# Attention and token MLP on one core: when GpSimd gets its turn on the port that it shares with VectorE

## Chip, cores and metric

The kernel runs on one core of one Trainium2 chip. The metric is the device time in microseconds of one execution; the time of a kernel is the median of several runs. Five engines work beside each other: TensorE (PE in the profile, its weight loads PEld), VectorE (DVE), ScalarE (ACT), GpSimd (POOL) and SyncE (SP), which issues the DMAs.

## What is computed

The input x is 2048 x 512 in bf16. It is normalized by rows once (`xn`). The output is x plus two terms of it:

```python
xn  = layernorm(x)
# A: full attention, 32 heads of 16 elements, 2048 queries and keys
p   = softmax(q @ k.T * 16 ** -0.5);  A = concat(p @ v) @ wo
# B: a token MLP (2048 -> 1376 -> 2048) over the transposed, once more normalized xn
u   = gelu(einsum("bsd,sf->bdf", layernorm(xn), w1) + b1)
B   = (einsum("bdf,fs->bds", u, w2) + b2).T
out = x + A + B
```

The bulk of the work is the exponential of 32 x 2048 x 2048 scores, 134 million of them.

## The kernel before

**Tiles.** The scores are cut into 1024 tiles of 128 keys x 1024 columns (two heads times 512 queries). For each tile TensorE makes the scores (line 798) into two PSUM banks, one engine takes the exponential into a buffer (`pT`, or a part of `x_sb` that has come free), and TensorE multiplies the buffer by the values (line 880). Sums and products are gathered in one PSUM bank for 32 tiles (a block), then copied out (line 1102), divided and projected.

**Two ways to the exponential.** Most tiles go to ScalarE, which has an exponential (line 824). The others go to VectorE: one pass adds a constant to the scaled score and writes it as an int16 that is read as bf16 (`dexp`, line 833, PSUM to SBUF). Its error is taken down by three more copies of the buffer, each shifted by another constant (`SHIFTS`, line 839, int16, SBUF to SBUF); all four are multiplied by the values and summed in PSUM. So a tile on VectorE costs one `dexp`, three shifts and four products where a tile on ScalarE costs one exponential and one product. Each of the three shifts can run on VectorE (`shd`) or on GpSimd (`shp`). A `dexp` or an exponential is written as one record of 1024 columns where the two banks are neighbours, else as two of 512.

**The order.** Nothing of the order is written out by hand. When the program is built, a planner (`Sched` and the loop that ends the kernel function) keeps a modelled clock of each engine, lists what could be issued next on every engine with an estimated start (`est`), and adds the earliest. Costs are pairs: the time until the engine takes its next instruction, and the time until the result is there (`SH_I, SH_L = 1.11, 1.05` for a shift on GpSimd, `TS_I, TS_L = 0.335, 0.42` for one on VectorE). A semaphore is taken as `SEM = 0.05`. What the planner added becomes each engine's instruction stream, with the semaphore waits that the dependencies need.

**Choices of the planner.** Eight numbers steer it (`POLICIES`, 36 rows), among them `d_steal`, the lead that lets a tile go to VectorE, and `p_slack`. `PLAN` names one row of them for each 16 tiles, 64 in all. A piece of work is a candidate for GpSimd only if the next moment at which VectorE could want the port lies far enough behind the estimated start on GpSimd:

```python
pl = [z for z in pl if max(dve_port, sc.free["dve"]) - z[0] >= z[4] - p_slack]
```

`z[0]` is the estimated start and `z[4]` the length that is asked for (`SH_I` for a shift, 1.25 for other GpSimd work).

**The port.** Shifts on VectorE, one late multiply on VectorE and all computing instructions on GpSimd are marked as users of one port. In the model VectorE's marked instruction starts no earlier than the start of GpSimd's last one plus its issue time, and GpSimd's no earlier than the end of the issue time of VectorE's last one plus `POOL_AFTER = 0.03` (`port_time`). In the program GpSimd's instruction also gets a dependency on VectorE's last marked instruction (`port_op`): it waits on a semaphore until that one has finished. VectorE has no wait in the other direction.

Of the kernel before, what the change touches and what calls it, by code (L numbers as in the profile page):

```python
# [58 lines left out]
SEM = 0.05  # L59
PE_SWITCH = 0.10  # L60
PE_LAT = 0.38
PV_T = 0.1095
POOL_AFTER = 0.03
AS_I, AS_L = 0.8, 0.9
EXP_I, EXP_L = 0.904, 1.03
EXPH_I, EXPH_L = 0.477, 0.60
# [16 lines left out]
SH_I, SH_L = 1.11, 1.05  # L83
# [12 lines left out]
PLAN_STEP = 16  # L96
PLAN = tuple(int(c, 36) for c in "00f41j96ioe4283j88076r8jjti283fos8rs08tig23g0ih10n7tg0i05608f5v6")
URGENT = ("kv0", "qt", "kt", "vt")
URG_DUE = 24
UT0, UT_STEP = 196, 31  # L100
# [8 lines left out]
class Op:  # L109
# [3 lines left out]
    def __init__(self, eng, fn, name=""):  # L113
        self.eng = eng
        self.fn = fn
        self.pos = -1
        self.deps = []
        self.signals = False
        self.waits = []
        self.is_dma = False  # L120
        self.dma_sem = None
        self.dma_val = 0
        self.q = None
        self.after = None
        self.name = name
        self.t0 = 0.0
        self.t1 = 0.0


class Sched:  # L130
    ENGS = ("pe", "act", "dve", "pool", "sp")

    def __init__(self, nc, es):
        self.nc = nc
        self.es = es
        self.streams = {e: [] for e in self.ENGS}
        self.order = []
        self.last_writer = {}
        self.readers = {}
        self.dma_ops = []  # L140
        self.free = {e: 0.0 if e in ("sp", "act") else 0.7 for e in self.ENGS}
        self.busy = {e: 0.0 for e in self.ENGS}
        self.pe_mode = None
        self.pe_end = 0.0
        self.pe_tiles = {}
        self.port_free = {"dve": 0.0, "pool": 0.0}
        self.port_op = None
        self.act_end = 0.0
        self.pe_work = []
        self.filler = None  # L150
        self.pend = []
# [85 lines left out]

    def port_time(self, eng, t):

        return max(t, self.port_free["pool"] if eng == "dve" else self.port_free["dve"] + POOL_AFTER)  # L240

    def _time(self, op, cost, ready, port):
        eng = op.eng
        if port:
            ready = self.port_time(eng, max(self.free[eng], ready))
        if op.is_dma:
            op.t0 = max(self.free[eng], ready)
            self.free[eng] = op.t0 + cost[0]
            op.t1 = op.t0 + cost[1]
        elif eng == "pe":  # L250
            mode, tiles, dur = cost
            t = max(self.free["pe"], ready)
            if mode != self.pe_mode:
                t = max(t, self.pe_end + PE_SWITCH)
                self.pe_mode = mode
                self.pe_tiles = {}
            for x in tiles:
                t = max(t, self.pe_tiles.get(x, 0.0))
            for x in tiles:
                self.pe_tiles[x] = t + dur  # L260
            self.pe_end = max(self.pe_end, t + dur)
            self.free["pe"] = t + 0.004
            self.busy["pe"] += dur * len(tiles) / 4.0
            op.t0, op.t1 = t, t + dur + PE_LAT - 0.214
            self.pe_work.append((t, dur, len(tiles) / 4.0))
        else:
            op.t0 = max(self.free[eng], ready)
            self.free[eng] = op.t0 + cost[0]
            self.busy[eng] += cost[0]
            op.t1 = op.t0 + cost[1]  # L270
            if eng == "act":
                op.t1 = max(op.t1, self.act_end + cost[0] + (EXP_GAP if op.name == "exp" else 0.0))
                self.act_end = op.t1
                self.free[eng] = max(self.free[eng], op.t1 - ACT_QUEUE)
        if port:
            self.port_free[eng] = op.t0 + cost[0]

    def add(self, eng, fn, reads=(), writes=(), name="", dma=False, out_dma=False, cost=None, port=None):
        op = Op(eng, fn, name)
        op.is_dma = dma  # L280
        op.q = "o" if out_dma else "i"
        if cost is None:
            cost = (DMA_I, DMA_L) if dma else (("F", (0, 1, 2, 3), 0.22) if eng == "pe" else (EV_I, EV_L))
        deps = self._deps(eng, reads, writes, dma)
        deps.discard(op)
        if port is None:
            port = eng == "pool" and not dma
        ready = self.ready(eng, reads, writes, dma)
        if eng == "pe" and self.filler is not None:
            self.pend = [k[1] for k in writes if k[0] == "bank"] if name == "sc" and cost[2] > 0.2 else []  # L290
            self.keep_clock(ready, cost)
        self._time(op, cost, ready, port)
        if port and eng == "pool" and self.port_op is not None:
            deps.add(self.port_op)
        if port and eng == "dve":
            self.port_op = op
        op.deps = list(deps)
        for k in reads:
            self.readers.setdefault(k, []).append(op)
        for k in writes:  # L300
            self.last_writer[k] = op
            self.readers[k] = []
        op.pos = len(self.streams[eng])
        self.streams[eng].append(op)
        self.order.append(op)
        if dma:
            self.dma_ops.append(op)
        return op
# [79 lines left out]
def bass_parallel_sum__softmax_full_mha__mixer_token_mlp__prompt_kernel(  # L388
# [18 lines left out]
    with ExitStack() as es:  # L407
# [415 lines left out]
        def exp_specs(n):  # L823
            return [dict(eng="act", fn=lambda e, cs=cs, src=src: e.activation(buf(pbuf[n])[:, cs], src, ACTF.Exp, scale=LN2_128),  # L824
                         reads=[("bank", k) for k in ks], writes=half_keys(free_p[0], cs), name="exp",
                         cost=(EXP_I, EXP_L) if side(n) else (EXPH_I, EXPH_L)) for cs, src, ks in parts(n)]
# [5 lines left out]
        def dexp_spec(n, w):  # L832
            return [dict(eng="dve", fn=lambda e, cs=cs, src=src: e.tensor_scalar(  # L833
                buf_i(w)[:, cs], src, IBIAS, 0.0, ALU.add, ALU.max),
                reads=[("bank", k) for k in ks], writes=half_keys(w, cs), name="dexp",
                cost=(P1_I, P1_L) if side(n) else (P1H_I, P1H_L)) for cs, src, ks in parts(n)]
# [491 lines left out]
        def h_ok():  # L1328
            return next_n >= H_AT + H_STEP * h_n[0] and all(("xT", t) in have for t in range(NT))
# [45 lines left out]
        def est(specs):  # L1375
            s0 = specs[0]
            r = 0.0
            for s_ in specs:
                r = max(r, sc.ready(s_["eng"], s_["reads"], s_["writes"]))
            t = max(sc.free[s0["eng"]], r)  # L1380
            if s0.get("port"):
                t = sc.port_time(s0["eng"], t)
            return t
# [102 lines left out]
        while True:  # L1486
            if next_n >= plan_at and plan_at < NN:
                d_steal, p_keep, dead_slack, pe_fit, ext_rank, d_back, d_fly, p_slack = POLICIES[PLAN[plan_at // PLAN_STEP]]
                plan_at += PLAN_STEP
# [11 lines left out]
            if ready_q and free_p:  # L1501
                el = []
                for n in ready_q:
                    sp_ = exp_specs(n)
# [6 lines left out]
            if ready_q and fly < d_fly and len(free_p) >= 4 + p_keep:  # L1511
                act_free = sc.free["act"]
                for qi, n in enumerate(ready_q):
                    if NN - n <= D_END:
                        continue
                    sp_ = dexp_spec(n, free_p[0])
                    t = est(sp_)
# [6 lines left out]
            for j in sh_jobs:  # L1524
                if j["ok"]():
                    sp_ = shift_spec("dve", j["w"], j["o"], j["k"])
# [11 lines left out]
            pl = []  # L1538
            dve_port = min([z[0] for z in dl if z[2] == "shd" or (z[2] == "gen" and z[3]["cur"][1][0].get("port"))] + [1e9])
            for j in sh_jobs:  # L1540
                if NN - j["n"] <= POOL_END:
                    continue
                sp_ = shift_spec("pool", j["w"], j["o"], j["k"])
                pl.append((est([sp_]), 1, "shp", (j, sp_), SH_I))
            for g in frees + exts:
                if g["cur"] and g["cur"][0] == "pool":
                    pl.append((est(g["cur"][1]), 0, "gen", g, 1.25))
            if hgen is not None and h_ok():
                pl.append((max(sc.free["pool"], next_h), 2, "h", None, 0.67))
            pl = [z for z in pl if max(dve_port, sc.free["dve"]) - z[0] >= z[4] - p_slack]  # L1550
# [6 lines left out]
            sp_, e_s = None, 1e9  # L1557
# [3 lines left out]
            if next_n < NN and pv_grp >= grp(vblk(next_n)) - 1 and len(free_banks) >= 2 + spare and score_has(next_n):  # L1561
                s_ = best_pair()
                banks_of[next_n] = s_
                sp_ = score_specs(next_n)
# [44 lines left out]
            if not cands:  # L1609
                pl = [z for z in ([] if not sh_jobs else [(0, 0, "shd", (sh_jobs[0], shift_spec("dve", sh_jobs[0]["w"], sh_jobs[0]["o"], sh_jobs[0]["k"])))])]  # L1610
# [12 lines left out]
            elif kind == "exp":  # L1623
                n, sp_ = what
                ready_q.remove(n)
                exp_commit(n)
                for z in sp_:
                    add(z)
                free_banks.extend(banks_of[n])
            elif kind == "dexp":  # L1630
                n, sp_ = what
# [3 lines left out]
                for z in sp_:  # L1635
                    add(z)
# [8 lines left out]
            elif kind in ("shd", "shp"):  # L1645
                j, sp_ = what
# [15 lines left out]
            elif kind == "gen":  # L1662
                g = what
# [9 lines left out]
            elif kind == "score":  # L1673
                n, sp_, s_ = what
# [6 lines left out]
            elif kind == "pv":  # L1681
# [4 lines left out]
                if pv_left[b] == 0:  # L1686
                    g = dict(gen=task_spill() if b < 0 else task_epilogue(b) if b < NBLK - 1 else task_tail(b - NBLK + 1), cur=None)
# [4 lines left out]
            elif kind == "ext":  # L1692
                g = what
# [21 lines left out]
            for i, (rel, due, nm, gen, need) in enumerate(ext_tasks):  # L1715
# [19 lines left out]
                g = dict(gen=gen, cur=None, due=due, name=nm)  # L1735
# [63 lines left out]
```

## Time and profile before

| what | value |
|---|---|
| median of 3 runs | 699.4 us (699.33 to 699.7) |
| profiled execution, whole time | 698.69 us |
| its span, first to last instruction | 696.9 us |
| granted TensorE clock | 1.000 |
| busy: PE, DVE, ACT, POOL | 686.0, 664.7, 678.5, 388.0 us |
| shifts on POOL (line 839) | 303 records, 1043 ns each |
| shifts on DVE (line 839) | 609 records |
| `dexp` on DVE (line 833) | 233 of 1024 columns, 142 of 512 |

The whole time of the profiled execution is 1.8 us over its span and 0.7 us under the median of the runs. A group of the profile names line, engine, operation, what is written and read, the number of records, busy time and mean duration, then the idle time of the engine just before these records and what ended most of it. Records of one engine overlap by some 85 ns, since an instruction starts before the one ahead has written its last results: a shift on VectorE has a record of 420 ns and the next instruction starts 334 ns after it.

### The profile page before, as it was taken

How to read it: one execution, taken by the hardware profiler on the slowest of the kernel's cores; microseconds unless marked ns; L12 is line 12 of the kernel's file. 1: busy time of each engine (PE TensorE's matmuls, PEld its weight loads, DVE VectorE, ACT ScalarE, POOL GpSimd, SP SyncE). 2: the span in 40 equal slices, each digit the busy share in tenths (PEclk: the TensorE clock that was granted, in tenths of full speed). 3: DMA queues.
4: the chain of work that ended last, by engine and by line, in shares of the span. 5: the costliest groups of instructions: out<-in, count | busy, mean ns of one | idle time of the engine just before them, and what ended most of it. 6: DMA issues, size and time to landing. Idle time of an engine off the chain costs nothing.

```text
span 696.9 us, 30015 instructions
## 1 busy us (share of the span) xinstructions
PE 686.0 (98%) x13235; PEld 317.9 (46%) x13235; DVE 664.7 (95%) x1198; ACT 678.5 (97%) x789; POOL 388.0 (56%) x436
## 2 busy tenths in 40 slices
PE   8999999999999999999999999999999999999998
PEld 6544444444444444444444444444444444444444
DVE  7888979989999999998999999999999999989997
ACT  7999999999999999999999999999999999999996
POOL 6856744355565556555555565555555545545644
PEclk9999999999999999999999999999999999999999
DMA  7410140101222121221122213120220202112101
GB/s 227 68 24 12 50 83 20 30 3 32 43 47 57 40 59 41 49 56 35 28 49 63 59 30 81 45 50 27 48 61 24 49 23 64 46 46 62 41 26 46
DMA packets 88756, 33.86 MB, mean 49 GB/s; under 512 B 70514, under 2 KB 88626, under 8 KB 88626
## 3 DMA queue, kind: packets, MB, share of 16 engines
q1 hardware_dynamic: 87810, 31.56, 19.6%
q8 instruction: 103, 1.69, 1.0%
q10 hardware_dynamic: 816, 0.39, 0.2%
q14 instruction: 27, 0.22, 0.1%
HBM read 21.70 MB, written 2.35 MB: 35 GB/s over the span
## 4 chain that ended last, share of the span: by engine, by line
PE 66%; DVE 23%; ACT 9%; issue 2%; POOL 0%; DVEq 0%; POOLq 0%
PE ps L880 23%; PE ps L798 23%; PE ps L928 16%; DVE pT L833 9%; ACT pT L824 7%; DVE pT L839 6%; DVE x_sb L833 3%; DVE x_sb L839 2%; ACT x_sb L824 2%; PE ps L984 1%; DVE OT L1102 1%; PE ps L869 0%; DVE Qall L954 0%; DVE osb L1076 0%; PE ps L721 0%
## 5 line engine op out<-in xcount | busy, mean ns | idle before, releaser
L824 ACT ACTIVATE pT<-ps 128x1024 bf16<-128x1024 f32 (+1 forms) x570 | 528.5, 1106 | 5.4 <-PE ps L798 4.6
L798 PE MATMUL ps<-QT,KT 32*128 32x512 bf16 x1976 | 276.0, 385 | 1.9 <-DVE pT L833 0.4
L833 DVE TENSOR_SCALAR pT<-ps 128x1024 int16<-128x1024 f32 (+1 forms) x265 | 264.1, 1013 | 9.9 <-PE ps L798 9.6
L880 PE MATMUL ps<-pT,V 128*32 128x256 bf16 x4624 | 245.1, 275 | 1.4 <-DVE OT L1102 0.3
L839 POOL TENSOR_SCALAR pT<-pT 128x1024 int16<-128x1024 int16 x158 | 164.8, 1043 | 124.2 <-DVE pT L839 86.6
L824 ACT ACTIVATE x_sb<-ps 128x1024 bf16<-128x1024 f32 (+1 forms) x197 | 201.3, 1089 | 1.2 <-PE ps L798 1.2
L798 PEld LDWEIGHTS ps<-QT,KT 32*128 32x128 bf16 x1976 | 76.9, 91 | 169.8 <-ACT pT L824 72.8
L880 PEld LDWEIGHTS ps<-pT,V 128*32 128x32 bf16 x4624 | 111.5, 96 | 73.7 <-issue 52.7
L839 DVE TENSOR_SCALAR pT<-pT 128x1024 int16<-128x1024 int16 x317 | 129.4, 434 | 0.4
L833 DVE TENSOR_SCALAR x_sb<-ps 128x1024 int16<-128x1024 f32 (+1 forms) x110 | 110.9, 1024 | 2.7 <-PE ps L798 1.8
L880 PE MATMUL ps<-x_sb,V 128*32 128x256 bf16 x1712 | 109.2, 275 | 0.4 <-DVE x_sb L839 0.3
L839 POOL TENSOR_SCALAR pT<-x_sb 128x1024 int16<-128x1024 int16 x64 | 66.8, 1043 | 50.0 <-DVE pT L839 39.0
L839 POOL TENSOR_SCALAR x_sb<-pT 128x1024 int16<-128x1024 int16 x57 | 59.5, 1043 | 37.7 <-DVE pT L839 26.8
L880 PE MATMUL ps<-pT,VM 128*32 128x256 bf16 x912 | 64.8, 275 | 0.9 <-POOL VM L687 0.5
L928 PE MATMUL ps<-hx,wblk 128*32 128x512 bf16 x688 | 59.9, 384 | 0.0
L880 PEld LDWEIGHTS ps<-x_sb,V 128*32 128x32 bf16 x1712 | 43.8, 96 | 25.4 <-issue 19.5
L839 DVE TENSOR_SCALAR pT<-x_sb 128x1024 int16<-128x1024 int16 x133 | 54.5, 432 | 0.2
L839 DVE TENSOR_SCALAR x_sb<-pT 128x1024 int16<-128x1024 int16 x110 | 46.1, 426 | 0.1
L928 PE MATMUL ps<-wkv_raw,wblk 128*32 128x512 bf16 x512 | 44.7, 385 | 0.0
L1141 POOL TENSOR_TENSOR oT<-oC,denb 128x256 bf16<-128x256 f32 (+1 forms) x32 | 23.3, 729 | 31.0 <-DVE pT L839 16.2
L839 POOL TENSOR_SCALAR x_sb<-x_sb 128x1024 int16<-128x1024 int16 x24 | 25.0, 1043 | 18.5 <-DVE pT L839 15.6
L880 PEld LDWEIGHTS ps<-pT,VM 128*32 128x32 bf16 x912 | 24.2, 96 | 15.6 <-issue 9.7
(124 smaller groups left out, 462.3 us busy)
## 6 DMA issues: line engine op xcount, KB each, us to landing
wblk<-in_B_w_dram SPq DMA_DIRECT2D x10, 512.0 KB, 4.6
wblk<-in_B_w_dram SPq DMA_DIRECT2D x16, 320.0 KB, 3.6
oC<-OT SPq DMA_DIRECT2D x248, 16.0 KB, 2.2
denb<-rden_scratch SPq DMA_DIRECT2D x124, 32.0 KB, 1.9
xr<-in_A_x_dram SPq DMA_DIRECT2D x16, 128.0 KB, 2.4
out_dram<-osb SPq DMA_DIRECT2D x16, 128.0 KB, 2.0
QT<-Qall SPq DMA_DIRECT2D x120, 16.0 KB, 1.8
x_sb<-in_A_x_dram SPq DMA_DIRECT2D x2, 512.0 KB
```

The source lines that it names most:

```text
L798: specs.append(dict(eng="pe", fn=lambda e, r=r, bk=bk: e.matmul(bank(bk), lhsT=KT[32 * r:32 * r + 32, T, 128 * kt:128 * (kt + 1)], rhs=QT[ ...
L824: return [dict(eng="act", fn=lambda e, cs=cs, src=src: e.activation(buf(pbuf[n])[:, cs], src, ACTF.Exp, scale=LN2_128), reads=[("bank", k) ...
L833: return [dict(eng="dve", fn=lambda e, cs=cs, src=src: e.tensor_scalar(buf_i(w)[:, cs], src, IBIAS, 0.0, ALU.add, ALU.max), reads=[("bank" ...
L839: return dict(eng=eng, fn=lambda e: e.tensor_scalar(buf_i(o), buf_i(w), float(SHIFTS[k]), 1.0, ALU.add, ALU.mult), reads=[("pT", w), ("pTh ...
L880: specs.append(dict(eng="pe", fn=lambda e, c=c, h=h, i=i, off=off: e.matmul(bank(pv_bank[vb])[32 * c:32 * c + 32, 256 * par:256 * par + 25 ...
L928: specs.append(dict(eng="pe", fn=lambda e, c=c, w=w: e.matmul(bank(ex)[32 * c:32 * c + w, :], lhsT=lhs_of(32 * c, 32 * c + w), rhs=rhs, st ...
L984: specs.append(dict(eng="pe", fn=lambda e, ct=ct, c=c, i=i, t=t: e.matmul(bank(ex)[32 * c:32 * c + 32, 128 * i:128 * (i + 1)], lhsT=xnT[:, ...
L1102: yield "pvev", [dict(eng="dve", name="pvev", fn=lambda e: e.tensor_copy(OT32[:, eb, :], bank(pv_bank[b])), reads=[("bank", pv_bank[b])], ...
L1141: yield "pool", [dict(eng="pool", fn=lambda e, cs=cs: e.tensor_tensor(oT[0:m, qb % NOT, T, cs], oC32[0:m, tb_, cs], denb[0:m, tb_, cs], AL ...
```

## The change

Three things change together.

- GpSimd's dependency moves. When a port user is added on VectorE and the model has it starting right behind the instruction in front of it (less than 0.03 us after VectorE was free), GpSimd's next instruction depends on that instruction in front, and not on the port user itself. Otherwise it depends on the port user as before. VectorE's stream is in order, so the instruction in front ends first.
- The model's times of the port change. GpSimd may start 0.05 + 0.03 us after the end of the instruction that it depends on, and no earlier than 0.165 us (`PORT_EARLY`) before the port user's issue time is over. VectorE may start 0.14 us (`PORT_DVE`) before GpSimd's result is there: 0.91 us after the start of a GpSimd shift, where it was 1.11. The length that a candidate for GpSimd must find free goes from 1.11 to 0.91 for a shift and from 1.25 to 1.05 for other work.
- `PLAN` is another table: 61 of its 64 entries differ.

```diff
-POOL_AFTER = 0.03
+POOL_AFTER, PORT_EARLY, PORT_DVE = 0.03, 0.165, 0.14
...
-PLAN = tuple(int(c, 36) for c in "00f41j96ioe4283j88076r8jjti283fos8rs08tig23g0ih10n7tg0i05608f5v6")
+PLAN = tuple(int(c, 36) for c in "0u389ydi80tnddje715t8t8z40i0d08h0n2h5fuv8188so0yz7xncr0rf83ij8o0")
...
     def port_time(self, eng, t):
-        return max(t, self.port_free["pool"] if eng == "dve" else self.port_free["dve"] + POOL_AFTER)
+        if eng == "dve":
+            return max(t, self.port_free["pool"])
+        if self.port_dep is not None:
+            t = max(t, self.port_dep.t1 + SEM + POOL_AFTER)
+        return max(t, self.port_free["dve"] - PORT_EARLY)
...
         if port:
-            self.port_free[eng] = op.t0 + cost[0]
+            self.port_free[eng] = op.t0 + (cost[0] if eng == "dve" else cost[1] - PORT_DVE)
...
+        was_free = self.free[eng]
         self._time(op, cost, ready, port)
-        if port and eng == "pool" and self.port_op is not None:
-            deps.add(self.port_op)
+        if port and eng == "pool" and self.port_dep is not None:
+            deps.add(self.port_dep)
         if port and eng == "dve":
-            self.port_op = op
+            st = self.streams["dve"]
+            self.port_dep = st[-1] if st and op.t0 - was_free < 0.03 else op
...
-                pl.append((est([sp_]), 1, "shp", (j, sp_), SH_I))
+                pl.append((est([sp_]), 1, "shp", (j, sp_), SH_L - PORT_DVE))
...
-                    pl.append((est(g["cur"][1]), 0, "gen", g, 1.25))
+                    pl.append((est(g["cur"][1]), 0, "gen", g, 1.05))
```

More of the change, by code (lines that the diff above doesn't have):

```diff
@@ L146, in __init__ @@
         self.port_free = {"dve": 0.0, "pool": 0.0}
-        self.port_op = None
+        self.port_dep = None
         self.act_end = 0.0
```

## The prediction

> **What bounds the kernel now.** I began with the busy times by stage (the table of windows: busy time of each engine, PE, PEld, DVE, ACT, POOL in that order, then granted clock, DMA share and GB/s).
>
> ```profile
> 20.00:160.00 140.00, 136.64 (x2964) 66.96 (x2966) 126.88 (x239) 139.18 (x175) 79.98 (x105) 1.00 0.17 36
> 160.00:660.00 500.00, 498.61 (x9316) 221.92 (x9314) 490.67 (x856) 495.32 (x560) 277.63 (x274) 1.00 0.20 47
> 660.00:696.90 36.90, 32.97 (x670) 16.44 (x662) 32.08 (x59) 28.87 (x32) 17.59 (x19) 1.00 0.13 37
> ```
>
> Through 500 of the 697 us ScalarE is busy for 99% and VectorE for 98%; GpSimd has 222 us free. TensorE shows 99.7%, but the ends of its records are modelled and overlap, so I asked the waits who holds it up:
>
> ```profile
> PEld ps L798 <- ACT pT L824: 72.8, 284, 0.5
> PEld ps L798 <- DVE pT L833: 28.3, 104, 0.5
> PEld ps L798 <- ACT x_sb L824: 22.0, 86, 0.4
> PEld ps L798 <- DVE x_sb L833: 12.6, 46, 0.5
> ```
>
> The weight loads of the scores waited 136 us in sum for exponentials to free their banks. So TensorE waits for ScalarE and VectorE together, although the chain that ended last gives it 66%. The time is the exponentials that these two must share: it falls if VectorE can take more tiles, and VectorE can if it loses fewer microseconds elsewhere. The groups show where it spends them:
>
> ```profile
> L833 DVE TENSOR_SCALAR pT<-ps 128x1024 int16<-128x1024 f32 x163 | 198.7, 1219 | 7.2 <-PE ps L798 6.8
> L839 DVE TENSOR_SCALAR pT<-pT 128x1024 int16<-128x1024 int16 x317 | 129.4, 434 | 0.4
> L839 POOL TENSOR_SCALAR pT<-pT 128x1024 int16<-128x1024 int16 x158 | 164.8, 1043 | 124.2 <-DVE pT L839 86.6 <-DVE x_sb L839 30.1 <-DVE pT L833 3.4
> ```
>
> 304 tiles went to VectorE (233 whole, 142 halves); of their 912 shifts 609 ran on VectorE and 303 on GpSimd. GpSimd's idle time ends almost always with a VectorE shift: that is the turn on the port.
>
> **The price of VectorE time.** Start to start, a `dexp` of 1024 columns takes VectorE 1.133 us, a shift 0.334, an exponential ScalarE 0.903 (medians of the records). A tile moved from ScalarE to VectorE, with two of its shifts there, costs VectorE 1.133 + 2 x 0.334 = 1.80 and frees 0.903 on ScalarE. Both are full, so f us freed on VectorE let f / (1.80 + 0.903) more tiles move, and the time falls by 0.903 of that: f / 3.0. Within 0.2% (1.4 us) of the time before is what a measurement of this kernel can't tell from no change.
>
> **The handoff as traced.** The usual cycle (timeline of GpSimd, then of VectorE; start, duration):
>
> ```profile
> 399.71 1.04 POOL L839 TENSOR_SCALAR x_sb<-pT 128x1024 int16<-128x1024 int16 x1 [0.76 <-DVE pT L839]
> 401.51 1.04 POOL L839 TENSOR_SCALAR x_sb<-x_sb 128x1024 int16<-128x1024 int16 x1 [0.76 <-DVE pT L839]
> ...
> 400.68 0.75 DVE L839 TENSOR_SCALAR pT<-x_sb 128x1024 int16<-128x1024 int16 x2
> 401.35 1.22 DVE L833 TENSOR_SCALAR pT<-ps 128x1024 int16<-128x1024 f32 x1
> ```
>
> The two shifts end at 401.43, GpSimd begins at 401.51: 82 ns, as for 254 of its instructions after 20 us. In 248 of these the shift had followed its predecessor without a pause (starts overlap ends by 85 ns), and the predecessor's end lay 333 to 338 ns earlier (10th to 90th percentile) than the semaphore used now. So **the wait moves by 0.334 us**, and GpSimd arrives 0.168 us after VectorE's shift has begun, while it runs.
>
> What happens to one that arrives so is in the trace, where other GpSimd work came in during a shift (GpSimd's row, then VectorE's):
>
> ```profile
> 47.40 0.75 POOL L687 TENSOR_SCALAR VM<-V 128x544 bf16<-128x544 bf16 x1 [0.78 <-DVE V L994]
> ...
> 47.23 0.42 DVE L839 TENSOR_SCALAR pT<-pT 128x1024 int16<-128x1024 int16 x1
> ```
>
> It arrived 168 ns into the shift and took 748 ns; the median of that line is 644. Another (line 634, at 85.19) took 792 against 692. VectorE's shifts kept 0.42 us. So arriving early stretches GpSimd's record by 0.10 us and costs VectorE nothing. A GpSimd shift, counted from the start of VectorE's shift, now ends at 0.42 + 0.082 + 1.043 = 1.545 us and would end at 0.168 + 1.043 + 0.10 = 1.311: 0.234 earlier.
>
> In the other direction, the 28 VectorE shifts with records over 440 ns all started under a running GpSimd instruction and ended 278 to 284 ns after it: as if they began 0.14 before its end. That is the new `PORT_DVE`; the old model had VectorE wait 0.2 us too long. These 28 lost 8.9 us.
>
> **Window sums.** Between two VectorE shifts lies other work, a window. A GpSimd shift fits one without holding VectorE up if the window is 1.545 - 0.14 - 0.334 = 1.07 us long now, and 0.84 after; each further shift needs 1.123 (back to back, median). I cut VectorE's records after 25 us into their 608 windows (375 GpSimd instructions are in them).
>
> - *Blocked shifts.* 14 of the 28 stood behind a GpSimd chain whose first instruction had the 82 ns handoff; ending 0.234 sooner takes off some 0.2 us each: 2.8 us of VectorE. All 28: 6.2. None: 0.
> - *Room without blocking.* The windows hold 346 GpSimd shifts by the old need and 356 by the new: 10 shifts leave VectorE, 10 x 0.334 = 3.3 us. If the planner finds none: 0.
> - *Room with a short block.* If VectorE may be held up by 0.25 us the windows hold 404, that is 48 more, nearly all in windows of one 0.6 us copy. Each blocks 0.84 - 0.60 = 0.24 and saves 0.334, 0.10 net. The new filter lets these in (with slack 0.5 it asks for 0.41 us; the copy gives 0.77), the old one did not (0.61 asked, 0.58 given). Not each will have a shift at hand; I take a third: 1.6 us. Ends 0 and 4.8.
> - *The moved wait itself:* 0.33 us earlier on an engine with 222 us free is worth nothing on the path, and nothing is queued behind it on GpSimd but the next such piece (it issues no DMA). Cover is that idle time; without it each handoff would gain 0.234.
> - *More products:* each tile that moves adds three sets of four products on TensorE, about 0.11 us a set; for 3 tiles 1 us. I cost it at nothing because the score loads wait 136 us for exponentials; if that cover is gone, 1 us is added.
>
> Sum: 2.8 + 3.3 + 1.6 = 7.7 us of VectorE, 2.6 us of time. The profiled execution would go from 698.69 to 696.1; it lay 0.7 under the median, so the median would be 696.8. By the ends: half of the first term alone, 0.5 us (698.9); all at their upper ends 14.3 / 3.0 = 4.8 us (694.6).
>
> **Rivals.**
>
> 1. *GpSimd let in too eagerly* (slower). With slack 0.8 the new filter asks for 0.11 us; one VectorE shift ahead already gives 0.165, so GpSimd may take the port with no other VectorE work as cover. VectorE is then free at 0.334 and the port at 1.311 - 0.14 = 1.17: blocked 0.84, saved 0.334, 0.50 lost. Four of the table's 64 entries have slack 0.8: 64 tiles, some 19 on VectorE, so up to 9.5 us. With slack 0.5 a reciprocal (16 in the kernel, 0.26) suffices: 0.24 lost each, 3.9 us. Together 4.5 us of time, less 2.6 gained: 701.3. It decides from some 15 such turns on (7.7 / 0.50). Against: the planner prices the block and takes a `dexp` instead where scores lie ready. Chance 0.12.
> 2. *The port is held until VectorE's shift has fully ended* (no gain, or slower). GpSimd's work then begins no earlier than now, the window need stays at 1.07, and the planner is 0.23 too hopeful: first term 0; 10 x (0.334 - 0.23) = 1.0; 16 x (0.10 - 0.23) = -2.1, or -6.2 for all 48. Time 699.8 to 701.1. Against: the row at 47.40, whose work ended 500 ns after the shift's end where it needs 644, so it began 144 ns before that end. Chance 0.06. The Trainium skill has this rule (SBUF — State Buffer, section "A bandwidth-pool intuition that's wrong (but worth ruling out)"): GpSimd blocked by VectorE goes on about 115 ns after VectorE's end, measured on descriptor writing. By that figure, an estimate, the new handoff would be 33 ns worse than the 82 of now, and the sum nothing or below; this trace disagrees, by those 144 ns.
> 3. *The reordering opens other waits* (slower). 61 table entries differ, so every later choice differs. After 20 us VectorE has 48 waits over 100 ns, 23.3 us, mostly for scores and projections; half as many again is 11.7 / 3.0 = 3.9 us: 700.7. A third fewer would give 694.2. Chance of the bad side 0.12.
> 4. *No change.* GpSimd starts earlier and idles later, the planner moves no shifts: 699.4. For it: GpSimd already had 222 us free and left them. Chance 0.10.
>
> GpSimd overtaking the shift it should follow would block VectorE for 0.9 us, but needs VectorE's shift to start over 82 ns after its predecessor; none of 609 started more than 36 ns after. No chance of its own.
>
> **Numbers.** The forecast, with its better side, has 0.60: 696.8. Slower is rivals 1, 2 and 3, 0.30; same is rival 4, 0.10. The range goes from 692.5 (all upper ends and most of a third fewer waits: 694.6 - 2.1) to 701.3 (rival 1), with 1 in 10 beyond each.
>
> **What would show it.** Right: GpSimd's shifts begin about 0.17 us after a VectorE shift's start, with records near 1.14 us; over 303 of them; more than 304 tiles on VectorE and fewer ScalarE exponentials; records over 440 ns on VectorE losing less than 8.9 us. Rival 1 shows as many records near 1.2 us on VectorE's shifts; rival 2 as GpSimd records near 1.3; rival 3 as VectorE idle time well over 30 us in sum (30.0 now). I am wrong if shifts move to GpSimd and the tiles on VectorE do not grow, or if ScalarE is no longer 99% busy between 160 and 660 us.

## The result, and the profile after

| | before | changed |
|---|---|---|
| median | 699.37 us | 703.6 us |
| ratio, 95% interval | | 1.006 (1.0048 to 1.0073) |
| span of the profiled execution | 696.9 us | 702.2 us |
| shifts on GpSimd / VectorE | 303 / 609 | 344 / 568 |
| tiles on VectorE | 304 | 304 |
| VectorE shifts with records over 440 ns (blocked), time lost | 28, 8.9 us | 68, 23.0 us |
| VectorE idle, from the span's start to its last instruction | 30.0 us | 34.6 us |
| whole exponentials on ScalarE, mean start to start | 665, 930.3 ns | 679, 936.7 ns |

The kernel became 0.6% slower. (Blocked time is what a record has over 418 ns, summed.) The same table of windows as before, of the changed kernel:

```profile
20.00:160.00 140.00, 136.38 (x2970) 66.55 (x2974) 130.42 (x242) 138.38 (x173) 94.85 (x117) 1.00 0.17 35
160.00:660.00 500.00, 495.18 (x9274) 219.19 (x9266) 482.44 (x777) 494.21 (x542) 325.27 (x301) 1.00 0.20 47
660.00:702.20 42.20, 37.79 (x770) 18.04 (x770) 38.57 (x71) 34.67 (x39) 23.38 (x23) 1.00 0.12 32
```

GpSimd, the fifth engine of each row, works 48 us more between 160 and 660 us; TensorE, VectorE and ScalarE all work less there. What GpSimd took over did not turn into more work of the others. (The busy time of TensorE is modelled; that of the other engines is recorded.) The groups of the changed kernel, as before by line, engine and shape:

```profile
L839 DVE TENSOR_SCALAR pT<-ps 128x1024 int16<-128x1024 f32 x173 | 210.2, 1215 | 4.4 <-PE ps L804 4.2
L845 DVE TENSOR_SCALAR pT<-pT 128x1024 int16<-128x1024 int16 x292 | 127.5, 461 | 0.9
L845 POOL TENSOR_SCALAR pT<-pT 128x1024 int16<-128x1024 int16 x174 | 192.3, 1105 | 92.0 <-DVE pT L845 52.2 <-DVE x_sb L845 18.4 <-PE ps L804 7.7
```

VectorE's shifts went from 317 to 292 in this group, but their mean from 434 to 461 ns, so they cost nearly the same. GpSimd's mean went from 1043 to 1105 ns. The timeline shows both (GpSimd's rows, then VectorE's):

```profile
82.66 1.04 POOL L845 TENSOR_SCALAR pT<-x_sb 128x1024 int16<-128x1024 int16 x1
84.06 1.15 POOL L845 TENSOR_SCALAR pT<-x_sb 128x1024 int16<-128x1024 int16 x1 [0.36 <-DVE pT L845]
...
81.96 1.21 DVE L839 TENSOR_SCALAR pT<-ps 128x1024 int16<-128x1024 f32 x1
83.09 1.22 DVE L845 TENSOR_SCALAR pT<-x_sb 128x1024 int16<-128x1024 int16 x2
84.23 1.21 DVE L839 TENSOR_SCALAR x_sb<-ps 128x1024 int16<-128x1024 f32 x1
```

The two shifts at 83.09 take 1.22 us where two free ones take 0.75: the first stands behind GpSimd's instruction of 82.66 to 83.70. The second then lets GpSimd in at 84.06, and that record is 1.15 us. Of 344 GpSimd shifts 206 arrived 0.14 to 0.26 us into a VectorE shift; their median record is 1.152 us.

Who held up the score loads (waits: total, number, longest):

```profile
PEld ps L804 <- ACT pT L830: 56.7, 212, 0.5
PEld ps L804 <- DVE pT L839: 30.8, 96, 0.8
PEld ps L804 <- ACT x_sb L830: 21.1, 83, 0.4
PEld ps L804 <- DVE x_sb L839: 18.3, 55, 0.6
```

For ScalarE they waited 77.8 us instead of 94.8, for VectorE 49.1 instead of 40.9. And the chain that ended last, by engine, of the kernel before and of the changed one:

```profile
PE 66%; DVE 23%; ACT 9%; issue 2%; POOL 0%; DVEq 0%; POOLq 0%
```

```profile
PE 54%; DVE 33%; ACT 6%; POOL 5%; issue 2%; POOLq 0%; DVEq 0%
```

VectorE's share rose from 23 to 33%, GpSimd's from 0 to 5%. So VectorE now runs late, and ScalarE waits for scores: a whole exponential usually starts 0.904 us after a whole one ahead of it. One that started over 20 ns later than that was released by a score matmul 76 times before (14.1 us of delay) and 118 times now (18.1 us). In the mean whole exponentials start 6.4 ns further apart, 679 x 6.4 = 4.3 us of the 5.3 us of the span. That the scores were late because VectorE freed their banks late is argued from the waits and the chain; it was not followed from score to score.

### The profile page after: what moved, and what is told of

The parts are those of the page before. It is cut to its first block, busy times and chain, and to the rows that moved or that the text cites. A ratio compares the mean times of both kernels' runs of the same rounds, so it can differ in the third digit from the quotient of the medians.

```text
span 702.2 us, 30075 instructions
## 1 busy us (share of the span) xinstructions
PE 687.0 (98%) x13283; PEld 316.8 (45%) x13283; DVE 665.4 (95%) x1132; ACT 681.5 (97%) x775; POOL 455.5 (65%) x477
## 4 chain that ended last, share of the span: by engine, by line
PE 54%; DVE 33%; ACT 6%; POOL 5%; issue 2%; POOLq 0%; DVEq 0%
PE ps L886 19%; PE ps L804 19%; PE ps L934 14%; DVE pT L839 13%; DVE pT L845 8%; DVE x_sb L839 6%; ACT pT L830 4%; DVE x_sb L845 2%; PE ps L990 1%; ACT x_sb L830 1%; POOL pT L845 1%; POOL mv L1246 1%; DVE OT L1108 1%; POOL hx L1251 1%; PE ps L708 0%
## 5 line engine op out<-in xcount | busy, mean ns | idle before, releaser
L830 ACT ACTIVATE pT<-ps 128x1024 bf16<-128x1024 f32 (+1 forms) x549 | 505.2, 1045 | 5.4 <-PE ps L804 4.5
L839 DVE TENSOR_SCALAR pT<-ps 128x1024 int16<-128x1024 f32 (+1 forms) x245 | 256.0, 1058 | 8.9 <-PE ps L804 8.7
L845 POOL TENSOR_SCALAR pT<-pT 128x1024 int16<-128x1024 int16 x174 | 192.3, 1105 | 92.0 <-DVE pT L845 52.2
L830 ACT ACTIVATE x_sb<-ps 128x1024 bf16<-128x1024 f32 (+1 forms) x204 | 208.1, 1068 | 2.2 <-PE ps L804 2.0
L839 DVE TENSOR_SCALAR x_sb<-ps 128x1024 int16<-128x1024 f32 (+1 forms) x105 | 116.2, 1114 | 6.2 <-PE ps L804 5.7
L845 POOL TENSOR_SCALAR pT<-x_sb 128x1024 int16<-128x1024 int16 x83 | 91.3, 1100 | 45.0 <-DVE pT L845 26.8
L845 POOL TENSOR_SCALAR x_sb<-pT 128x1024 int16<-128x1024 int16 x64 | 71.3, 1114 | 35.2 <-DVE pT L845 22.7
L845 DVE TENSOR_SCALAR pT<-x_sb 128x1024 int16<-128x1024 int16 x142 | 60.6, 453 | 0.3
L886 PEld LDWEIGHTS ps<-x_sb,V 128*32 128x32 bf16 x1720 | 43.9, 96 | 27.4 <-issue 20.9
L934 PE MATMUL ps<-hx,wblk 128*32 128x512 bf16 x688 | 56.0, 384 | 0.0
L845 DVE TENSOR_SCALAR x_sb<-pT 128x1024 int16<-128x1024 int16 x97 | 40.8, 432 | 0.2
L886 PEld LDWEIGHTS ps<-pT,VM 128*32 128x32 bf16 x904 | 24.0, 96 | 14.8 <-issue 9.7
```

Source lines behind the costliest of these rows:

```text
L845: return dict(eng=eng, fn=lambda e: e.tensor_scalar(buf_i(o), buf_i(w), float(SHIFTS[k]), 1.0, ALU.add, ALU.mult), reads=[("pT", w), ("pTh ...
L886: specs.append(dict(eng="pe", fn=lambda e, c=c, h=h, i=i, off=off: e.matmul(bank(pv_bank[vb])[32 * c:32 * c + 32, 256 * par:256 * par + 25 ...
L934: specs.append(dict(eng="pe", fn=lambda e, c=c, w=w: e.matmul(bank(ex)[32 * c:32 * c + w, :], lhsT=lhs_of(32 * c, 32 * c + w), rhs=rhs, st ...
```

## Experiments

Three theories. **S**: the planner's new port times are 0.10 us too hopeful. `PORT_EARLY` 0.165 says that GpSimd's work starts when its instruction arrives; on the chip the record is stretched (1.152 against 1.043), so each order planned with it has VectorE late. **T**: the rules are sound and the new table is a bad pick. **W**: the moved wait itself costs time. The runs were taken in several sessions, in which the kernel before had medians of 699.4 to 699.9 us; a difference between sessions is good to about 0.5 us.

### The moved wait alone, in the order of before

```diff
# before.py, planned times untouched, so the order is untouched
-            deps.add(self.port_op)
+            deps.add(self.port_dep)
...
+            self.port_dep = st[-1] if st and op.t0 - was_free < 0.03 else op
```

> The order of before, instruction by instruction, with nothing changed but the semaphore that GpSimd waits for (the VectorE instruction in front of the port's last user). Theory W (the moved wait itself costs): 702 us or more, with VectorE's shift records longer. Theories S and T: 698 to 699.6 us; GpSimd arrives about 0.17 us after a shift's start, its records are near 1.15 us instead of 1.043, their ends come about 0.23 us sooner, and the 8.9 us of blocked VectorE time fall to 5 to 8 us.

Measured: 699.65 us against 699.7, ratio 0.9996 (0.9984 to 1.0008). 221 GpSimd shifts arrived under a VectorE shift (median 0.168 us in, record 1.155, end 1.323 us after that shift's start). Blocked VectorE time fell from 8.9 to 6.1 us. The groups:

```profile
L842 DVE TENSOR_SCALAR pT<-pT 128x1024 int16<-128x1024 int16 x317 | 128.5, 431 | 0.4
L842 POOL TENSOR_SCALAR pT<-pT 128x1024 int16<-128x1024 int16 x158 | 177.9, 1126 | 109.7 <-DVE pT L842 64.9 <-DVE x_sb L842 27.0 <-DVE pT L836 5.4
```

Same counts as before; GpSimd's mean is 83 ns longer, VectorE's 3 ns shorter. W falls: it asked for 702 us or more. By the interval the wait alone is worth between 1.1 us of gain and 0.6 us of loss.

### The old wait, in the order of the changed kernel

```diff
# after.py, order untouched
-            deps.add(self.port_dep)
+            deps.add(self.port_op)      # VectorE's last port user itself
...
+            self.port_op = op
```

> The order of the changed kernel, instruction by instruction, with GpSimd waiting for the port user itself again. GpSimd's records are 1.043 us once more, but start 0.33 us and end 0.23 us later. Theory W: faster than the changed kernel by 2 us or more, under 701.6 us. Theory S (the order has no room for the port's later release): blocked time of VectorE rises over the 23.0 us of the changed kernel to 30 us or more, and the time to 705 to 715 us. Theory T: somewhat over 703.6 us.

Measured: 715.89 us, ratio 1.0226 (1.021 to 1.0241); 69 blocked shifts, 33.7 us.

```profile
L847 DVE TENSOR_SCALAR pT<-pT 128x1024 int16<-128x1024 int16 x292 | 133.0, 479 | 0.9
L847 POOL TENSOR_SCALAR pT<-pT 128x1024 int16<-128x1024 int16 x174 | 182.4, 1048 | 106.4 <-DVE pT L847 72.5 <-DVE x_sb L847 20.8 <-PE ps L806 3.8
```

GpSimd's records are short again (1048 ns), so the stretch belongs to arriving under a shift. But each end comes later, VectorE's mean rises from 461 to 479 ns, and with 10.7 us more blocking the kernel took 12.3 us more. W falls again (it asked for under 701.6 us); S had the blocked time right and the time 0.9 us too low at its upper end. This order has no slack at the port: what the port is late there, the kernel is late.

### Tables and rules exchanged

The changed rules with the old table, and the old rules with the new table (only the `PLAN` line is exchanged).

> The change with the table of before. Theory S (the planner doesn't know that a GpSimd instruction which arrives under a VectorE shift takes 0.10 us longer; it packs VectorE's shifts too tightly behind GpSimd, and they block): the blocked time of VectorE's shifts stays far over the 8.9 us of before, 18 us or more, and the time is over that of the changed kernel, 705 to 712 us, since this table was not chosen for the new rules. Theory T (the new table is a bad pick, the rules are sound): about 697 to 700 us. Theory W (the moved wait itself costs time on the chip, whatever the order): 703 us or more, not told apart here.

> The kernel before with the table of the change, the wait and the port times as they were. Theory T (the table is the cause): 703 to 705 us. Theory S: the blocked time of VectorE's shifts stays near 9 us (under 14), and the time says only that a table fits the rules it was chosen under: 704 to 712 us. Theory W: nothing in particular.

Measured: 711.27 us (1.0162, 1.0145 to 1.0179; 75 blocked shifts, 25.5 us) and 711.34 us (1.0167, 1.0152 to 1.0182; 30 blocked, 9.4 us). T expected 697 to 700 us of the first and 703 to 705 of the second; both miss. S has both inside its ranges, of time and of blocked time. Each table is better under the rules that it came with: by 12 us under the old ones (711.34 to 699.7), by 7.7 under the new (711.27 to 703.6). So a comparison of rules needs a table chosen for neither.

### One row for all 64 places, three sets of rules

```diff
# after.py; in before.py the PLAN line alone
-PLAN = tuple(int(c, 36) for c in "0u389ydi80tn...")
+PLAN = tuple(int(c, 36) for c in "0000000000...")     # then "8888888888..."
# third set only
-POOL_AFTER, PORT_EARLY, PORT_DVE = 0.03, 0.165, 0.14
+POOL_AFTER, PORT_EARLY, PORT_DVE = 0.03, 0.06, 0.14
```

> The rules of before (old wait, old port times) with a flat table: row 0 of the policies in all 64 places, so that no table was picked for any rules. It is the base of the next two: some 707 to 712 us, with VectorE's shifts blocked for 5 to 15 us.

> The changed rules (moved wait, PORT_EARLY 0.165) with the same flat table. Theory S (the turn is planned 0.10 us too early, since GpSimd's record is 1.15 us where it arrives under a shift and the planner has 1.05): 709 to 715 us, not faster than the flat table under the rules of before by more than 1 us, VectorE blocked for 18 us or more. Theory T (the rules are sound and only the table is a bad pick): 2 to 5 us faster than the flat table under the rules of before, 704 to 708 us.

> As the one before with one number changed: PORT_EARLY 0.06 instead of 0.165, so that the planner has GpSimd's instruction begin 0.105 us later behind a VectorE shift, which is what its record is stretched by. Theory S: 2 to 8 us faster than with 0.165, 704 to 709 us, and 1 us or more faster than the flat table under the rules of before. Theory T: within 1.5 us of the run with 0.165.

> A second draw of the flat comparison, since any change of a planned time reorders all that follows: row 8 of the policies in all 64 places, with the rules of before. Base of the next two: 707 to 713 us.

> Row 8 in all places with the changed rules (PORT_EARLY 0.165). Theory S (the turn is planned 0.10 us too early): within 2 us of the same table under the rules of before, or slower. Theory T (the rules are sound, the new table a bad pick): 2 us or more faster than it. VectorE blocked for 18 us or more in both.

> As the one before with PORT_EARLY 0.06. Theory S: faster than with 0.165 by 2 us or more, as it was by 3.0 us with row 0. If that difference was the chance of one reordering: anything from 3 us slower to 3 us faster.

| flat table | rules of before | changed, 0.165 | changed, 0.06 |
|---|---|---|---|
| row 0, us | 710.79 | 711.6 | 708.62 |
| row 0, ratio to the kernel before | 1.0161 (1.0144 to 1.0178) | 1.0171 (1.0156 to 1.0186) | 1.0136 (1.0119 to 1.0153) |
| row 8, us | 713.4 | 715.82 | 710.74 |
| row 8, ratio | 1.0196 (1.0181 to 1.0211) | 1.023 (1.0213 to 1.0247) | 1.0161 (1.0146 to 1.0176) |
| VectorE blocked, row 0 / row 8, us | 11.7 / 10.2 | 20.9 / 18.4 | 18.9 / 16.7 |
| tiles on VectorE, row 0 / row 8 | 298 / 307 | 301 / 317 | 296 / 315 |

With 0.165 the rules bring nothing or a loss (row 8, +2.4 us); 0.105 us later in that one number takes 3.0 and 5.1 us off. T would have had the rules with 0.165 2 us or more ahead of those of before; neither draw shows that. Row 8 under the rules of before came out 0.4 us over the range expected of it. The blocked time fell by only 2 us each: with 0.06 VectorE is still blocked for longer than under the old rules, but when it was meant to be (the planned blocking stands in the table below). The chain that ended last changes in row 8. With 0.165:

```profile
PE 45%; DVE 44%; ACT 3%; POOL 3%; issue 3%; SPq 1%; DMA 1%; DVEq 0%; POOLq 0%
```

and with 0.06:

```profile
PE 46%; DVE 26%; ACT 24%; POOL 2%; issue 2%; DVEq 0%; POOLq 0%
```

VectorE carries 44% and ScalarE 3% in the first; in the second they have 26 and 24%, though 315 tiles run on VectorE against 317. In row 0 it is not so: VectorE's share rises there from 23 to 30% with 0.06. The row 0 gain over the rules of before (2.2 us) has intervals that touch; in row 8 (2.7 us) they do not.

### The number mended, and a table chosen for it

`PORT_EARLY` 0.06 as above and another table, chosen by the planner's own end.

> The changed kernel with PORT_EARLY 0.06 and a table chosen anew for that value, by the planner's own end alone, on no chip. The planner ends it 0.4 us later than it ends the changed kernel with its table. Theory S (a turn planned 0.10 us too early is what the changed kernel loses): faster than the changed kernel's 703.6 us by 2 us or more, 697 to 701.5 us, although it is planned to end later. Theory T (only the choice of table counts): 703.5 to 705 us, as the planner's end says. Whether it beats the 699.4 us of before is open between 697 and 701.

Measured: 699.71 us, ratio to before 0.9998 (0.9989 to 1.0007): 3.9 us under the changed kernel. 333 shifts on GpSimd, 301 tiles on VectorE, 64 blocked shifts with 19.0 us, whole exponentials 926.6 ns apart. Its windows row and chain:

```profile
160.00:660.00 500.00, 498.35 (x9238) 216.84 (x9236) 484.31 (x798) 497.85 (x554) 315.50 (x291) 1.00 0.21 47
```

```profile
PE 63%; DVE 21%; ACT 12%; POOL 1%; issue 1%; POOLq 0%; DVEq 0%
```

ScalarE is busy for 497.9 of 500 us (494.2 in the changed kernel), and VectorE's share of the chain is back from 33 to 21%. T is out: planned to end 0.4 us later, it ends 3.9 us sooner. It is level with the kernel before, not better; no kernel run here is faster than that one by more than can be told.

Laying VectorE's starts in each trace beside the starts that the planner had given the same instructions shows the cause as a lag (median of those planned for 625 to 650 us). The same can be done for the blocked shifts, since the planner's clocks say which shifts it let the port hold up.

| kernel | planned end of VectorE, us | shifts blocked, planned / traced, us | lag, us |
|---|---|---|---|
| before | 693.6 | 11.3 / 8.9 | 0.05 |
| before, with the new table | 706.0 | 12.9 / 9.4 | 0.8 |
| row 0, rules of before | 704.0 | 16.9 / 11.7 | 2.0 |
| row 8, rules of before | 704.4 | 13.5 / 10.2 | 3.8 |
| changed (0.165) | 692.5 | 14.8 / 23.0 | 5.9 |
| changed, with the old table | 699.4 | 18.2 / 25.5 | 6.6 |
| row 0, 0.165 | 703.5 | 18.5 / 20.9 | 2.7 |
| row 8, 0.165 | 702.2 | 13.6 / 18.4 | 8.1 |
| row 0, 0.06 | 702.2 | 19.2 / 18.9 | 2.1 |
| row 8, 0.06 | 702.5 | 19.6 / 16.7 | 2.6 |
| 0.06 and a table of its own | 692.9 | 19.8 / 19.0 | 2.0 |

With 0.165 the chip blocks VectorE longer than planned in all four orders; with 0.06 and under the old rules the sums are below the plan in every order. Row 8 shows it most plainly: 0.165 and 0.06 are planned to end 0.3 us apart, and on the chip they are 5.1 us apart the other way. In row 0 the lags differ by only 0.6 us, so there most of the 3.0 us came with the other order that the planner then chose. The changed kernel was planned to end 1.1 us sooner than the one before and lags 5.9 us: 4.8 us, of which 4.2 were measured.

The lag is 1.7 us with only the wait moved and 15.6 with only the wait moved back. It is that of one execution, and good to about 1 us: the profiled execution with only the wait moved took 0.75 us more than its median, and 0.8 us of its lag was there within the first 45 us.

The old rules were wrong in both directions: GpSimd's start 0.14 us too early, VectorE's release behind GpSimd 0.2 us too late. Together they planned the release 1.475 us behind the start of VectorE's shift where it came at 1.405, 0.07 us too late. The change mended the second error and turned the first into another: 1.08 planned, 1.178 traced, 0.10 us too early.

## Why the prediction was wrong

The kernel was to become 0.4% faster and became 0.6% slower. The first of the two signs of being wrong came: 41 shifts moved to GpSimd and the tiles on VectorE stayed 304. The second did not: ScalarE is still 99% busy between 160 and 660 us.

**The handoff was right.** Arrival 0.168 us into the shift (measured 0.166), record 1.14 us (1.152), end 1.311 us after the shift's start (1.318), VectorE's shift unharmed (417 ns). With the wait alone the blocked time lost 2.8 us, the first term of the sum.

**Rival 2** (the port held to the shift's end) is out: that end at 1.318 leaves 0.142 us of GpSimd's 1.043 before VectorE's record ends at 0.417. The 115 ns behind VectorE's end that the Trainium skill states (SBUF — State Buffer, section "A bandwidth-pool intuition that's wrong (but worth ruling out)"), measured there on descriptor writing, don't hold for this pair of instructions.

**The term that failed is the room with a short block.** I let 26 shifts leave VectorE, 16 of them for 0.24 us of blocking each, and took 2.8 us of blocking off elsewhere: 7.7 us freed. 41 left, 41 x 0.334 = 13.7 us, and blocking rose by 14.1 us (8.9 to 23.0). In the place of +7.7 stands -0.4. Of the 68 blocks 35 cost more than the 0.334 us that a shift saves. Part of it the planner took on knowingly: it planned 14.8 us of blocking, where my terms make 9.9 (8.9 - 2.8 + 16 x 0.24); the other 8.2 us it did not plan. (The sign of less than 8.9 us that I gave for being right did not agree with these terms.)

**A term was missing.** My own sum had GpSimd's end at 1.311 us behind the shift's start; the rules of the diff plan it at 0.17 + 1.05 = 1.22. I priced a planner that is too hopeful in rival 2 (there by 0.23 us) and put this gap of 0.09 at nothing in the forecast, where about 200 instructions meet it. With the reordering that comes with it, mending it is worth 3.0 and 5.1 us under the flat tables, and 3.9 with a table of its own. With the order held, in the planner's own clocks: the changed kernel's order, timed once more with 0.06, ends 3.2 us later (695.78 against 692.54); row 8's ends 4.5 and row 0's 1.6 us later. That is a sum of the model and not a run, and it puts the changed kernel 2.2 us behind the 693.6 of before.

**f / 3.0 was no rule for a fixed order.** VectorE time freed behind the planner's back bought no time that can be told (moved wait alone: 2.8 us freed; the 0.9 us of the rule lie inside that interval, so they are not ruled out), while time lost there is paid in full and not by a third (old wait in the new order: 10.7 us, 12.3 of time). Only the planner turns freed time into tiles, and it had none to turn: 304 tiles before and after. It had itself planned a gain of only 1.1 us.

**Rival 1** (GpSimd let in too eagerly) named the right sign and the right victim, at 701.3 us, but not the place: its blocks of 0.84 us in four stretches of the table do not exist. The longest is 0.74, the mean 0.34, and the changed table has as many entries with slack 0.8 as the old one. **Rival 3** (other waits): VectorE's waits over 100 ns after 20 us rose from 23.3 to 25.9 us and not by half, and its idle time by 4.6 us; that goes with the lag. **Rival 4**: GpSimd did take more.

Left open: what the lag of about 2 us is that also orders without the 0.105 us keep (2.0 to 2.6 with 0.06, 2.0 and 3.8 in the flat tables under the old rules), and why the kernel before has none.

## What to carry to other kernels

Where an order is planned ahead, a size that is 0.1 us too hopeful at a resource that 200 instructions pass costs microseconds, and mending one of two errors that partly cancel lays the other bare: compare the traced start of each instruction with its planned one before a table is tuned. Compare rules under a table tuned for neither. Shifting work to an idle engine frees time only if the port that both need is free too.

## What the runs showed of the hardware

GpSimd arriving under a running VectorE shift is recorded from its arrival, and its record holds the wait (1.152 us instead of 1.043). It does not always get the next turn (changed kernel, GpSimd's row, then VectorE's):

```profile
85.54 1.05 POOL L640 TENSOR_SCALAR hx<-hx,mv 128x512 bf16<-128x512 bf16 x1 [0.33 <-DVE x_sb L839]
...
85.36 0.75 DVE L845 TENSOR_SCALAR pT<-x_sb 128x1024 int16<-128x1024 int16 x2
86.03 0.84 DVE L845 TENSOR_SCALAR x_sb<-pT 128x1024 int16<-128x1024 int16 x1
```

A GpSimd instruction that needs 691 ns arrived during a shift, a second VectorE shift followed without a pause and went first, and the record was 1049 ns; only the third shift waited (836 ns). The planner gives GpSimd the turn there. The trace of before has such a case too, at 93.47 us (1046 ns); the prediction's account of an early arrival rests on two others and leaves it out. The last kernel has two, at 76.05 and 109.37 us, where its lag is still 0.2 us, so its lag of 2.0 us has another source.
